# One order of ScalarE and VectorE work in a decoding step, and one more raw weight tile: attention with two feed-forward products on one core

## The chip, the cores and the metric

The kernel runs on one core of one Trainium2 chip. The core has TensorE for matmuls, VectorE and ScalarE for element-wise work, GpSimd, and SyncE, whose queue here issues all DMAs. Each engine takes its own instructions in the order in which the program puts them into its queue and waits on semaphores for the others. The metric is device time in microseconds (us) of one execution; lower is better.

## The reference

```python
x = softmax(q @ k^T / 8, causal) @ v          # 2 x 12 heads, 448 positions, 64 wide
x = x.reshape(896, 768)                       # tokens x model
h = max(x @ w1, x @ w2, x @ w3)               # 768 x 768 each
x2 = h @ w_out                                # 768 x 768
g = s * relu(x2 @ w_in) ** 2 + b              # 768 x 2048
out = g @ w_out2                              # 2048 x 768
```

q, k and v are float32. The weights are float64; the kernel gets their 64-bit words and makes a float32 value of each word itself.

## The kernel before

**Stages.** Attention works through 24 heads, a pair of heads at a time; `emit(t)` puts out the work of head `t` together with later work of the heads before it, in the order of the list `ORDER`. Then `moe()` follows: 36 products `x @ w1..w3` of 128 x 448 outputs (the first of them, `early_product`, is done during the last attention heads), 12 products `h @ w_out` (the x2 stage), 32 products `x2 @ w_in` (the g stage), and the output stage, line 559, with seven accumulators of 128 x 384 at a time, twice. A product is 6 x 3 matmuls of 448 columns (line 453): each operand is split into a high and a low part, and high x high, high x low and low x high are summed. Eight PSUM banks go round among the products; the output accumulators take the same eight in turn.

**Weight tiles.** There are 56, each 128 x 768. A tile goes through these operations: the DMA `wraw` (line 114); on ScalarE `wa` (line 133) and `wr` (line 134), which take the high and the low word apart; on VectorE two clamps (lines 137 and 140), then the rounding (lines 146 and 151); on ScalarE `whi` (line 156), the high part; on VectorE `wlo`, the difference (helper in line 86). Buffers: two for raw tiles, two for `wa`, two for `wr`, three for `whi` and `wlo`. A new raw tile is fetched into the buffer that line 146 has just read.

**Steps.** The decoding is cut into steps. `begin()` is called seven times in attention (at the heads in `STEPS`) and then once in each product, ahead of its last six-th of matmuls, and once for each f of the output stage. A call first puts out what is due from the products before it, then `decode()`. An even step ends with the rounding of one tile and `wa`, `wr` of the next; an odd step has `whi` and `wlo` of one tile and the clamps of the next. So one tile is started every two steps, and a product pair uses one tile.

**What is due in the g stage.** A product's evacuation is spread over the three steps that follow it: `relu` on ScalarE (line 544) from PSUM into `r`; then `stt` on VectorE (line 533), r = max(p, 0) * r, `ident` on ScalarE (line 536), s * r + b, and `copy` on ScalarE (line 539), the high part of g; then `sub` on VectorE (line 86), its low part. The buffers `r` come from the pool `tmp`, four in number. A step puts out the oldest first: `sub`, `stt`, `ident`, `copy`, `relu`. I use these names below: `wa`, `wr`, `whi`, `wlo`, clamps, rounding, and `sub`, `stt`, `ident`, `copy`, `relu`.

**SyncE's queue.** In attention it issues, for each pair of heads, the loads R and V, the store and the spread of the softmax sums (`rcd`, `rb`), and four copies QK; the first two raw tiles are fetched behind the head t = 17 (`FETCH`).

Of the kernel before, what the change touches and what calls it, by code (L numbers as in the profile page):

```python
# [27 lines left out]
)  # L28


FETCH = 17
STEPS = (19, 20, 21, 23, 24, 25, 27)
EARLY = {24: 2, 25: 2, 26: 1, 27: 1}

# [9 lines left out]
def kernel(  # L44
# [14 lines left out]
    nc = tc.nc  # L59
# [14 lines left out]
    const = ctx.enter_context(tc.tile_pool(name="const", bufs=1))  # L74
    x_p = ctx.enter_context(tc.tile_pool(name="x", bufs=KD))
    w_p = ctx.enter_context(tc.tile_pool(name="w", bufs=3))
    wr_p = ctx.enter_context(tc.tile_pool(name="wr", bufs=2))
    wa_p = ctx.enter_context(tc.tile_pool(name="wa", bufs=2))
    wd_p = ctx.enter_context(tc.tile_pool(name="wd", bufs=2))

    ident = const.tile([128, 128], F32, name="ident")
    sb = const.tile([128, 2], F32, name="sb")
    ones = const.tile([128, 512], mybir.dt.bfloat16, name="ones")

    def sub_lo(eng, lo, full, hi):
        eng.tensor_tensor(out=lo, in0=full, in1=hi.bitcast(F32), op=ALU.subtract)  # L86
# [8 lines left out]
    now = [0]  # L95
# [1 line left out]
    def after(steps, fn):  # L97
        due.setdefault(now[0] + steps, []).append((-steps, fn))

    def begin(enter=True):  # L100
        for _, fn in sorted(due.pop(now[0], []), key=lambda e: e[0]):
            fn()
        decode(enter)
        now[0] += 1

    step = begin

    w_src, raws, ready, stages = [], [], [], []

    def fetch_w():  # L110
        if w_src:
            src = w_src.pop(0)
            raw = wr_p.tile([128, DM], I64, tag="wraw", name="wraw")
            nc.sync.dma_start(out=raw, in_=src)
            raws.append(raw)

    def decode(enter=True):


        for fns in [s.pop(0) for s in stages]:  # L120
            for fn in fns:
                fn()
        while stages and not stages[0]:
            stages.pop(0)
        if not (enter and raws) or now[0] % 2:
            return
        raw = raws.pop(0)
        words = raw.bitcast(I32).rearrange("p (n t) -> p n t", t=2)
        low, high = (words[:, :, n] for n in range(2))
        a = wa_p.tile([128, DM], I32, tag="wa", name="wa")  # L130
        r = wd_p.tile([128, DM], I32, tag="wr", name="wr")
        f = a.bitcast(F32)
        nc.scalar.activation(out=f, in_=high.bitcast(F32), func=ACTF.Abs)  # L133
        nc.scalar.activation(out=r, in_=low.bitcast(U32), func=ACTF.Copy, scale=2.0 ** -29)  # L134

        def clamped():
            nc.vector.tensor_scalar(  # L137
                out=f, in0=f, scalar1=UNDER, scalar2=OVER, op0=ALU.max, op1=ALU.min
            )
            nc.vector.tensor_scalar(  # L140
                out=a, in0=a, scalar1=3, scalar2=0x3FFFFFF8,
                op0=ALU.logical_shift_left, op1=ALU.bitwise_and,
            )

        def rounded():
            nc.vector.scalar_tensor_tensor(  # L146
                out=a, in0=high, scalar=-0x40000000, in1=a,
                op0=ALU.bitwise_and, op1=ALU.bitwise_or,
            )
            fetch_w()  # L150
            nc.vector.tensor_tensor(out=a, in0=a, in1=r, op=ALU.add)  # L151

        def split():
            hi = w_p.tile([128, DM], F32R, tag="whi", name="whi")
            lo = w_p.tile([128, DM], F32R, tag="wlo", name="wlo")
            nc.scalar.copy(out=hi, in_=f)  # L156
            sub_lo(nc.vector, lo, f, hi)
            ready.append((hi, lo))

        stages.append([[clamped], [rounded], [split]])  # L160

    def next_w():
        return ready.pop(0)
# [6 lines left out]
    def attention():  # L170
        with ExitStack() as c2:
            pool = lambda n, b, **kw: c2.enter_context(tc.tile_pool(name=n, bufs=b, **kw))
            mask = pool("mk", 1).tile([CH, S], F32, name="mask")
            ld = pool("ld", 3)
            vp = pool("vp", 6)
# [204 lines left out]
            def emit(t):  # L380
# [47 lines left out]
                if t in EARLY:  # L428
                    ops["M"] = lambda: [next(first, None) for _ in range(EARLY[t])]
                ops["W"] = lambda: [begin() for at in STEPS if at == t]  # L430
                for n in ORDER[h]:
                    if n in ops:
                        ops[n]()

            for t in range(n_heads + 4):
                emit(t)
                if t == FETCH:
                    fetch_w()
                    fetch_w()
            for _ in first:  # L440
                pass


    t_p = ctx.enter_context(tc.tile_pool(name="tmp", bufs=4))
    early = {}

    def cols(dst, a, b):
# [125 lines left out]
    with tc.manual_schedule():  # L573
        attention()
        moe()
# [50 lines left out]
```

## Time and profile before

| | |
|---|---|
| runs, median (lowest to highest) | 565.22 us (563.42 to 567.94) |
| profiled execution | 562.34 us, its span 560.3 us |
| TensorE (PE) busy | 534.4 us, 95%; weight loads (PEld) 82% |
| VectorE (DVE), ScalarE (ACT), GpSimd (POOL) busy | 62%, 52%, 8% |
| mean granted TensorE clock | 0.991 |

The span runs from the first to the last instruction. A page of the profile gives busy shares for the whole span; which engine sets the pace in a stretch is read from views of that stretch: its busy time, the chain of waits that ended last, and the timeline of single instructions. In the timeline's rows the engine is named by its short name, L156 is line 156, and what stands in brackets is how long the engine stood idle before the row, and whose end released it.

### The profile page before, as it was taken

The page shows a single profiled execution, that of the slowest core. Times are in us where ns is not written, and L with a number is a line of the kernel's source. Part 1 is how long each engine was busy: PE and PEld are TensorE (multiplying, and loading weights), DVE is VectorE, ACT ScalarE, POOL GpSimd, SP SyncE. Part 2 cuts the span into 40 slices and gives each one's busy share as a digit, 9 for nine tenths or more (in the row PEclk, how much of TensorE's full clock was granted, in tenths as well). Part 3 has the DMA queues.
Part 4 walks back from the last instruction along what each step waited for, and adds up shares of the span by engine and source line. Part 5 has one row for each costly group of instructions (what it writes and reads, how often), then busy time and mean ns, then how long its engine had stood idle before and what let it go on. Part 6 is the DMA issues. An engine that isn't in the chain of part 4 may idle for free.

```text
span 560.3 us, 7507 instructions
## 1 busy us (share of the span) xinstructions
PE 534.4 (95%) x2788; PEld 457.8 (82%) x2789; DVE 348.1 (62%) x653; ACT 292.4 (52%) x574; POOL 47.2 (8%) x43
## 2 busy tenths in 40 slices
PE   8999999979999999999999999989887599999997
PEld 4666666558999999999999999867676599999997
DVE  5465566767757757667666575766757675556501
ACT  3777777954335344434444756657575643334201
POOL 3143535122000000000000000000000000000000
PEclk9999999999999999999999999999999699999999
DMA  8987877523333333233323322323132243253102
GB/s 205 214 245 193 220 183 239 160 85 114 113 112 113 112 113 113 73 124 107 104 105 109 114 70 100 94 75 112 57 113 61 109 135 125 99 191 117 54 0 99
DMA packets 21108, 68.43 MB, mean 122 GB/s; under 512 B 3088, under 2 KB 9744, under 8 KB 21072
## 3 DMA queue, kind: packets, MB, share of 16 engines
q1 hardware_dynamic: 21072, 67.95, 39.2%
q8 instruction: 22, 0.36, 0.3%
q14 instruction: 14, 0.11, 0.1%
HBM read 55.05 MB, written 2.80 MB: 103 GB/s over the span
## 4 chain that ended last, share of the span: by engine, by line
PE 71%; ACT 17%; DVE 8%; issue 2%; DMA 1%; SPq 0%; ACTq 0%
PE m L453 31%; PE m L559 21%; PE s L244 9%; PE t L309 5%; PE o L324 4%; ACT r L536 4%; ACT g L539 3%; DVE wlo L86 3%; ACT r L544 2%; ACT wa L133 2%; ACT wr L134 2%; ACT whi L156 2%; DVE g L86 2%; DVE r L533 2%; DVE wa L137 1%
## 5 line engine op out<-in xcount | busy, mean ns | idle before, releaser
L453 PE MATMUL m<-x,whi 128*128 128x448 f32 x816 | 233.1, 367 | 6.9 <-ACT whi L156 5.6
L453 PEld LDWEIGHTS m<-x,whi 128*128 128x128 f32 x816 | 152.3, 188 | 22.8 <-ACT whi L156 8.5
L453 PE MATMUL m<-x,wlo 128*128 128x448 f32 x408 | 149.9, 367 | 2.5 <-DVE wlo L86 2.5
L559 PE MATMUL m<-whi,g 128*128 128x384 f32 x448 | 116.7, 340 | 7.8 <-DVE r L533 7.0
L86 DVE TENSOR_TENSOR wlo<-wa,whi 128x768 fp32r<-128x768 f32 x56 | 53.8, 960 | 112.0 <-ACT whi L156 112.0
L559 PEld LDWEIGHTS m<-whi,g 128*128 128x128 f32 x448 | 82.5, 191 | 9.3 <-DVE r L533 8.1
L453 PEld LDWEIGHTS m<-x,wlo 128*128 128x128 f32 x408 | 76.6, 188 | 11.6 <-DVE wlo L86 5.6
L559 PE MATMUL m<-wlo,g 128*128 128x384 f32 x224 | 75.9, 339 | 0.5 <-DVE wlo L86 0.5
L133 ACT ACTIVATE wa<-wraw 128x768 f32<-128x768 f32 x56 | 51.0, 912 | 38.8 <-DMA wraw<-in_w_dram 22.7
L156 ACT CAST whi<-wa 128x768 fp32r<-128x768 f32 x56 | 46.6, 832 | 33.7 <-PE m L559 29.1
L252 DVE CUSTOM_DVE_ANT_0 s<-s,mask 112x224 f32<-112x224 f32 (+1 forms) x96 | 43.5, 455 | 27.2 <-PE s L244 26.2
L260 ACT ACTIVATE P<-s,mx 112x224 f32<-112x224 f32 (+1 forms) x96 | 46.9, 495 | 18.4 <-DVE mx L252 16.0
L151 DVE CUSTOM_DVE_ANT_0 wa<-wa,wr 128x1536 uint16<-128x1536 uint16 x56 | 54.7, 977 | 1.9
L146 DVE SCALAR_TENSOR_TENSOR wa<-wraw,wa 128x768 int32<-128x768 int32 x56 | 53.4, 953 | 0.6
L536 ACT ACTIVATE r<-r,sb 128x448 f32<-128x448 f32 x32 | 24.2, 758 | 50.0 <-DVE r L533 50.0
L134 ACT ACTIVATE wr<-wraw 128x768 int32<-128x768 uint32 x56 | 50.2, 896 | 0.0
L559 PEld LDWEIGHTS m<-wlo,g 128*128 128x128 f32 x224 | 42.8, 191 | 0.8 <-DVE wlo L86 0.8
L453 PE MATMUL m<-h,whi 128*128 128x448 f32 x144 | 40.9, 365 | 0.0
L397 ACT COPY PT<-t 112x336 f32<-112x336 f32 (+1 forms) x72 | 31.5, 477 | 12.0 <-PE t L309 12.0
L244 PE MATMUL s<-HL 64*112 64x224 f32 (+3 forms) x112 | 37.6, 364 | 0.2 <-DVE HL L86 0.2
L309 PE MATMUL t<-ident,P 112*112 112x112 f32 x240 | 32.8, 268 | 0.1
L244 PE MATMUL s<-QK 128*112 128x224 f32 (+1 forms) x88 | 32.7, 371 | 0.0
(48 smaller groups left out, 481.2 us busy)
## 6 DMA issues: line engine op xcount, KB each, us to landing
wraw<-in_w_dram SPq DMA_DIRECT2D x56, 768.0 KB
QK<-HL SPq DMA_DIRECT2D x44, 224.0 KB
R<-in_qk_dram SPq DMA_DIRECT2D x11, 448.0 KB
V<-in_v_dram SPq DMA_DIRECT2D x12, 224.0 KB
rb<-rcd SPq DMA_DIRECT2D x24, 112.0 KB
out_dram<-o SPq DMA_DIRECT2D x14, 192.0 KB
R<-in_qk_dram SPq DMA_DIRECT2D x2, 224.0 KB
rcd<-rows SPq DMA_DIRECT2D x12, 3.5 KB
```

Of the source, the lines that this page charges most:

```text
L86: eng.tensor_tensor(out=lo, in0=full, in1=hi.bitcast(F32), op=ALU.subtract)
L133: nc.scalar.activation(out=f, in_=high.bitcast(F32), func=ACTF.Abs)
L134: nc.scalar.activation(out=r, in_=low.bitcast(U32), func=ACTF.Copy, scale=2.0 ** -29)
L146: nc.vector.scalar_tensor_tensor(out=a, in0=high, scalar=-0x40000000, in1=a, op0=ALU.bitwise_and, op1=ALU.bitwise_or,)
L151: nc.vector.tensor_tensor(out=a, in0=a, in1=r, op=ALU.add)
L156: nc.scalar.copy(out=hi, in_=f)
L244: nc.tensor.matmul(ps[:, o:o + n], lhsT, rhs, start=(m == 0), stop=(m == len(terms) - 1))
L260: nc.scalar.activation(out=s_t["P"][:, poff[i]:poff[i] + n], in_=ps[:, o:o + n], func=ACTF.Exp, bias=s_t["mx"][:, i:i + 1], scale=-1.0, ac ...
L309: nc.tensor.transpose(ps[0:CH, o:o + CH], head[t]["P"][:, a:a + CH], ident[0:CH, 0:CH])
L453: nc.tensor.matmul(p, wt[w][:, ws], cols(act[i], a, b), start=(i == 0 and n == 0), stop=(i == len(act) - 1 and n == 2),)
L536: nc.scalar.activation(out=r, in_=r, func=ACTF.Identity, scale=sb[:, 0:1], bias=sb[:, 1:2])
L559: nc.tensor.matmul(acc[t][:, 0:EH], gt[f][:, a, ts], w[:, ws], start=(f == 0 and n == 0), stop=(f == KG - 1 and n == 2),)
```

## The change

In `decode()`, ScalarE's part of a step (`whi` of an odd step; `wa` and `wr` of an even one) is now put out ahead of what is due, and VectorE's part behind it as before, the newest tile first. So in an odd step the clamps now stand ahead of `wlo`. There are three raw buffers in place of two, and the first three raw tiles are fetched one by one behind the heads 16, 18 and 20. The pool `tmp` has three buffers in place of four, and the tile `ones` lies in attention's own space.

```diff
-FETCH = 17
+FETCH = (16, 18, 20)
...
-    wr_p = ctx.enter_context(tc.tile_pool(name="wr", bufs=2))
+    wr_p = ctx.enter_context(tc.tile_pool(name="wr", bufs=3))
...
-    def begin(enter=True):
+    def begin():
+        back = [f for f in [s.pop(0)() for s in stages] if f]
+        while stages and not stages[0]:
+            stages.pop(0)
+        if raws and now[0] % 2 == 0:
+            enter()
         for _, fn in sorted(due.pop(now[0], []), key=lambda e: e[0]):
             fn()
-        decode(enter)
+        for fn in reversed(back):
+            fn()
         now[0] += 1
...
-    def decode(enter=True):
-
-
-        for fns in [s.pop(0) for s in stages]:
-            for fn in fns:
-                fn()
-        while stages and not stages[0]:
-            stages.pop(0)
-        if not (enter and raws) or now[0] % 2:
-            return
+    def enter():
         raw = raws.pop(0)
...
             nc.scalar.copy(out=hi, in_=f)
-            sub_lo(nc.vector, lo, f, hi)
-            ready.append((hi, lo))
-
-        stages.append([[clamped], [rounded], [split]])
+
+            def low_part():
+                sub_lo(nc.vector, lo, f, hi)
+                ready.append((hi, lo))
+
+            return low_part
+
+        stages.append([lambda: clamped, lambda: rounded, split])
...
             for t in range(n_heads + 4):
                 emit(t)
-                if t == FETCH:
-                    fetch_w()
+                if t in FETCH:
                     fetch_w()
...
-    t_p = ctx.enter_context(tc.tile_pool(name="tmp", bufs=4))
+    t_p = ctx.enter_context(tc.tile_pool(name="tmp", bufs=3))
```

ScalarE's queue in the g stage, before, from the `whi` of an odd step over the even step to the next odd one's `whi` (a number behind a name tells one buffer's use from the next):

```order
L156 CAST whi_3683<-wa_3589 128x768
L536 ACTIVATE r_3661<-r_3661,sb_74 128x448
L539 CAST g_3628<-r_3661 128x448
L544 ACTIVATE r_3692<-m_3662 128x448
L133 ACTIVATE wa_3719<-wraw_3651 128x768
L134 ACTIVATE wr_3720<-wraw_3651 128x768
L536 ACTIVATE r_3692<-r_3692,sb_74 128x448
L539 CAST g_3628<-r_3692 128x448
L544 ACTIVATE r_3726<-m_3694 128x448
L156 CAST whi_3748<-wa_3654 128x768
```

The same queue and place now (the lines have moved by four: L152 is `whi`, L129 and L130 are `wa` and `wr`):

```order
L152 CAST whi_3684<-wa_3586 128x768
L536 ACTIVATE r_3633<-r_3633,sb_74 128x448
L539 CAST g_3569<-r_3633 128x448
L544 ACTIVATE r_3667<-m_3635 128x448
L129 ACTIVATE wa_3716<-wraw_3596 128x768
L130 ACTIVATE wr_3717<-wraw_3596 128x768
L536 ACTIVATE r_3667<-r_3667,sb_74 128x448
L539 CAST g_3634<-r_3667 128x448
L544 ACTIVATE r_3698<-m_3668 128x448
L152 CAST whi_3749<-wa_3651 128x768
```

The kinds follow one another as before. What moved is the place among the products: before, `ident`, `copy` and `relu` that follow `whi` belong to the next, even step, and now to the same odd step as `whi` (`whi_3684` and `relu` of product `m_3635` in place of `whi_3683` and `m_3662`, the product behind it). Likewise `wa`, `wr` now stand at the head of the even step and stood at its end.

VectorE's queue in the g stage, before, from the `wlo` of an odd step on:

```order
L86 TENSOR_TENSOR wlo_3229<-wa_3134,whi_3228 128x768
L137 TENSOR_SCALAR wa_3199<-wa_3199 128x768
L140 TENSOR_SCALAR wa_3199<-wa_3199 128x768
L86 TENSOR_TENSOR g_3108<-r_3172,g_3108 128x448
L533 SCALAR_TENSOR_TENSOR r_3206<-m_3174,r_3206 128x448
L146 SCALAR_TENSOR_TENSOR wa_3199<-wraw_3131,wa_3199 128x768
L151 ISA wa_3199<-wa_3199,wr_3200 128x1536
```

And now (L85 is the helper, L133 and L136 the clamps, L142 and L147 the rounding):

```order
L133 TENSOR_SCALAR wa_3196<-wa_3196 128x768
L136 TENSOR_SCALAR wa_3196<-wa_3196 128x768
L85 TENSOR_TENSOR wlo_3230<-wa_3131,whi_3229 128x768
L85 TENSOR_TENSOR g_3114<-r_3178,g_3114 128x448
L533 SCALAR_TENSOR_TENSOR r_3212<-m_3180,r_3212 128x448
L142 SCALAR_TENSOR_TENSOR wa_3196<-wraw_3076,wa_3196 128x768
L147 ISA wa_3196<-wa_3196,wr_3197 128x1536
```

The clamps and `wlo` have changed places; `sub` and `stt` and the rounding stand where they stood. On SyncE's queue the raw tiles behind heads 16, 18 and 20 now stand ahead of the spread `rb` and the QK copies of the next head; from the moe stages on the order is the same, each fetch two steps earlier with respect to the tile's use.

## Rows read from the trace of the kernel before

**Rows 1.** Chain that ended last, 120 to 305 us: start, us, what.

```profile
120.64 4.45 DMA wraw<-in_w_dram
...
127.34 175.39 PE m L453 x864
```

**Rows 2.** Timeline of ScalarE, g stage: start, us, engine, line, operation, [idle before].

```profile
311.63 0.82 ACT L156 CAST whi<-wa 128x768 fp32r<-128x768 f32 x1
315.61 0.76 ACT L536 ACTIVATE r<-r,sb 128x448 f32<-128x448 f32 x1 [3.16 <-DVE r L533]
316.41 0.57 ACT L539 CAST g<-r 128x448 fp32r<-128x448 f32 x1
316.88 0.54 ACT L544 ACTIVATE r<-m 128x448 f32<-128x448 f32 x1
317.32 0.89 ACT L133 ACTIVATE wa<-wraw 128x768 f32<-128x768 f32 x1
318.11 0.90 ACT L134 ACTIVATE wr<-wraw 128x768 int32<-128x768 uint32 x1
...
320.60 0.82 ACT L156 CAST whi<-wa 128x768 fp32r<-128x768 f32 x1
```

**Rows 3.** Timeline of VectorE in the same loop.

```profile
312.48 0.96 DVE L86 TENSOR_TENSOR wlo<-wa,whi 128x768 fp32r<-128x768 f32 x1 [2.94 <-ACT whi L156]
313.36 0.56 DVE L137 TENSOR_SCALAR wa<-wa 128x768 f32<-128x768 f32 x1
313.95 0.56 DVE L140 TENSOR_SCALAR wa<-wa 128x768 int32<-128x768 int32 x1
314.43 0.62 DVE L86 TENSOR_TENSOR g<-r,g 128x448 fp32r<-128x448 f32 x1
314.96 0.62 DVE L533 SCALAR_TENSOR_TENSOR r<-m,r 128x448 f32<-128x448 f32 x1
315.50 0.95 DVE L146 SCALAR_TENSOR_TENSOR wa<-wraw,wa 128x768 int32<-128x768 int32 x1
316.48 0.96 DVE L151 CUSTOM_DVE_ANT_0 wa<-wa,wr 128x1536 uint16<-128x1536 uint16 x1
```

**Rows 4.** Timeline of TensorE: first wait of the g stage, output stage.

```profile
358.33 0.47 PE L453 MATMUL m<-x,wlo 128*128 128x448 f32 x1 [0.31 <-DVE wlo L86]
...
429.04 0.45 PE L559 MATMUL m<-whi,g 128*128 128x384 f32 x1 [0.81 <-ACT whi L156]
...
441.11 0.69 PE L559 MATMUL m<-whi,g 128*128 128x384 f32 x1 [4.83 <-DVE r L533]
...
556.43 0.34 PE L559 MATMUL m<-whi,g 128*128 128x384 f32 x1
```

**Rows 5.** Stretches: length, busy PE, PEld, DVE, ACT, POOL, granted clock, DMA, GB/s.

```profile
365.00:380.00 15.00, 12.88 (x60) 10.51 (x59) 10.65 (x16) 8.58 (x15) 0.00 (x0) 1.00 0.16 53
440.00:455.00 15.00, 13.89 (x68) 13.89 (x69) 11.30 (x17) 8.70 (x12) 0.00 (x0) 0.82 0.30 105
450.00:550.00 100.00, 100.00 (x578) 100.00 (x578) 50.35 (x65) 31.43 (x39) 0.00 (x0) 1.00 0.29 101
```

**Rows 6.** Timeline of several engines, end of attention.

```profile
116.75 0.96 DVE L86 TENSOR_TENSOR wlo<-wa,whi 128x768 fp32r<-128x768 f32 x1 [2.62 <-ACT whi L156]
...
118.69 0.16 DVE L401 TENSOR_SCALAR su<-su 112x8 f32<-112x8 f32 x1
119.15 0.26 PE L282 MATMUL t<-ident,su 112*8 112x112 f32 x1 [2.83 <-DVE su L404]
...
125.18 0.91 ACT L133 ACTIVATE wa<-wraw 128x768 f32<-128x768 f32 x1 [2.75 <-DMA wraw<-in_w_dram]
...
127.34 0.68 PE L453 MATMUL m<-x,whi 128*128 128x448 f32 x2 [1.39 <-ACT t L462]
```

**Rows 7.** Timeline of SyncE and TensorE: QK of pair 10, issue and first use.

```profile
84.82 3.06 SPq L217 DMA_DIRECT2D QK<-HL  x4
...
95.89 0.34 PE L244 MATMUL s<-QK 128*112 128x224 f32 x1
```

More of the change, by code (lines that the diff above doesn't have):

```diff
@@ L82 @@
     sb = const.tile([128, 2], F32, name="sb")
-    ones = const.tile([128, 512], mybir.dt.bfloat16, name="ones")
     def sub_lo(eng, lo, full, hi):
@@ L98, in after @@
         due.setdefault(now[0] + steps, []).append((-steps, fn))
-    def begin(enter=True):
+    w_src, raws, ready, stages = [], [], [], []
+    def begin():
[4 more added lines that the diff above has]
+            enter()
         for _, fn in sorted(due.pop(now[0], []), key=lambda e: e[0]):
             fn()
-        decode(enter)
+        for fn in reversed(back):
+            fn()
         now[0] += 1
     step = begin
-    w_src, raws, ready, stages = [], [], [], []
     def fetch_w():
@@ L172, in attention @@
             pool = lambda n, b, **kw: c2.enter_context(tc.tile_pool(name=n, bufs=b, **kw))
+            ones = pool("on", 1).tile([128, 512], mybir.dt.bfloat16, name="ones")
             mask = pool("mk", 1).tile([CH, S], F32, name="mask")
```

## The prediction

> **What bounds the kernel now.** I read the page first (busy shares and slices), then the busy time by stretches, the chain of waits and, for the stretch where the chain leaves TensorE, the timelines of ScalarE and VectorE. The page says that TensorE is busy 95% of the span, so what can be won is the rest, and the question is where it lies.
>
> The chain answers it. From 127.34 us it is on TensorE alone for 864 matmuls, 0.2030 us each [rows 1]. That holds to 302.73 us, the entry to the g stage (the products `x2 @ w_in`). From there to 441 us the chain runs through ScalarE and VectorE in one repeating piece, two steps long: `whi`, `wlo`, the clamps, `stt` (line 533), `ident` (line 536), `copy` (539), `relu` (544), `wa`, `wr`, `ident`, `copy`, `relu`, `whi` [rows 2, 3]. Add the distances from start to start: `whi` to `wlo` 0.85, `wlo` 0.88, clamps 1.07 (0.59 + 0.48), `sub` 0.53, `stt` to `ident` 0.65, `ident`-`copy`-`relu` 1.71 (0.80 + 0.47 + 0.44), `wa` 0.79 and `wr` 0.80, the second `ident`-`copy`-`relu` 1.69; sum 8.97 us, which is the distance of the two `whi` at 311.63 and 320.60 [rows 2, 3]. TensorE needs 36 matmuls x 0.2030 = 7.31 us for the same two products. The loop is 1.66 us too slow, and it is slow by hand-over: ScalarE stands still 3.16 us in each loop, until `stt` [rows 2], and VectorE 2.94 us, until `whi` [rows 3].
>
> TensorE doesn't feel this at once, since weights and PSUM banks are ahead: its first wait of the stage is at 358.33 us [rows 4], 55.6 us or 6.2 loops after 302.73, so the lead is 6.2 x 1.66 = 10 us. After that it waits in every loop, and at the change to the output stage (line 559) for 4.83 us in one piece, behind which a matmul takes 0.69 us instead of 0.34 [rows 4]. The granted clock of 440 to 455 us is 0.82, that of 450 to 550 is 1.00 [rows 5]: behind the gap the engine runs for a while at 1.2 instead of 2.4 GHz.
>
> **What the gaps cost, counted by matmuls.** Products: 79 from 127.34 on, x 18 matmuls x 0.2030 = 288.7 us; the output stage starts at 429.04 [rows 1, 4], 301.7 us later. Lost: **13.0 us**. Output: 672 matmuls; 578 touch the 100 us of the window, about 2 of them at its edges, so 0.1736 us each [rows 5], 116.7 us in all; from 429.04 to the last matmul's end at about 556.6 [rows 4] are 127.6 us. Lost: **10.9 us**, low clock included.
>
> Idle time alone gives less: in 365 to 380 us the row has 2.12 us without a matmul, but 60 matmuls where 73.9 fit [rows 5], so 2.8 us are missing. The Trainium skill (Perfetto Trace Analysis, Identifying the Most-Contended Engine) says the same as a rule: matmul busy share is a poor measure, since pipelined instructions look smaller in the trace than they are. By idle time this sum would shrink by about a quarter, to 18 us instead of 23.9; the trace is on the side of the count.
>
> **The change, part by part.**
>
> *ScalarE's order.* No instruction is added or removed. In the g stage `whi` (odd steps) and `wa`, `wr` (even steps) move from behind `ident`, `copy`, `relu` to ahead of them. VectorE's clamps and rounding stay behind its other work, and only `wlo` and the clamps change places. Follow the new loop with the same distances, from `stt` of an odd step at 0, with no wait for TensorE. ScalarE: `ident` 0.65, `copy` 1.45, `relu` 1.92, free at 2.36. VectorE: clamps from 0.53, `wlo` 1.60 to 2.56 without a wait, because `whi` stood ahead of `ident`. Even step: `wa` waits for the buffer that `wlo` reads (a new wait) until 2.59, `wr` 3.38, `ident` 4.18 (its `stt` starts at 3.01 and is no obstacle), `copy` 4.96, `relu` 5.43. VectorE meanwhile rounds, 3.54 to 5.48. Then ScalarE's `whi` from 5.87; VectorE's `sub` when `copy` ends, 5.53, and `stt` at 6.06. The loop is **6.1 us**, under TensorE's 7.31. The lead isn't used up, nothing on TensorE is late, and the next thing to wait is ScalarE for TensorE, which costs nothing. A loop of up to 7.31 + 10/16 = 7.9 us would still cost nothing in the 16 loops of the stage.
>
> At the change of stage the seventh accumulator takes the bank of the last product but one. TensorE gets there 18 x 0.1736 = 3.1 us after the last product's end; with the engines in step, that bank's `stt` runs near that end. So the 4.83 us go, and the low clock with them. I take 13.0 + 10.9 = **23.9 us**. Bounds: nothing, if the loop stays at 8.97; 23.9 is all there is.
>
> *The new waits.* `wa` now stands ahead of `ident` and can be held by a raw tile not yet there or by `wlo`; queued behind it are `ident`, `copy`, `relu`, and VectorE's next `sub` and `stt` wait for those. In the sum it is held 0.23 us a loop (2.36 to 2.59).
>
> *VectorE's swap at the start.* At t = 23 `wlo` waits 2.62 us for `whi`, the clamps follow, and only then, at 118.69, the softmax sums, for whose transpose TensorE waits 2.83 us [rows 6]. With the clamps done in that wait the sums come 1.06 us sooner. *Third raw tile:* at 125.18 `wa` has waited 2.75 us for a transfer that could start only when VectorE let go of the buffer (4.45 us in the chain [rows 1]), and the evacuation behind it holds TensorE 1.39 us at 127.34 [rows 6]. With three tiles that raw is there long before; `wa` is then held by `wlo`, so I count some 0.5 of the 1.39. Together **1.6 us**; bounds 0 (the last attention head's x tile, made by GpSimd, could set the pace) and 1.06 + 1.39 = 2.45.
>
> *The early fetches.* The one after t = 16 goes on SyncE's queue ahead of the spread of the sums and the four QK copies, which were issued from 84.82 on for 3.06 us and are first read at 95.89 [rows 7]. A raw tile's 4.45 us [rows 1] fit in those 8 us: cost 0. Without that cover it is at most 4.45 us.
>
> *`tmp` 4 to 3, `ones` moved:* 0. The buffer that `relu` gets was last read by `sub` of three products before, one step earlier. The cover is that step; if it were gone, `relu` would wait one `sub`, 0.53 us.
>
> Sum: 560.3 - 23.9 - 1.6 = 534.8 us of span, and with the 2.0 us around it 536.8, against 562.34 of the profiled execution. The runs' median lies 2.9 us above that execution (565.22), so I forecast 536.8 + 2.9 = **540 us**.
>
> **The rivals.**
> *Part of it only.* The loop falls, but to between 7.9 and 8.97. Each 0.1 us above 7.9 costs 16 x 0.1 = 1.6 us; at 8.4 that is 8 us and most of the change of stage stays clean: 543 to 553. For it: `wa`'s new wait on `wlo`, and distances taken from a loop with pauses in it. Against: from 6.1 to 7.9 are 1.8 us of room.
> *The early raw fetch collides with QK.* TensorE waits up to 4.45 us near 96 us: 544. Against: the 8 us.
> *It doesn't do what it says.* Another loop of 9 us takes over, and only the start is won: 563. Against: the loop above has no such sum.
> *Slower: the head of ScalarE's queue blocks.* Place: `wa` in even steps, `whi` in odd ones. If each is held until VectorE has finished its whole step, the two engines alternate: ScalarE's 5.8 us (0.82 + 1.59 + 1.71 + 1.69) and VectorE's 5.9 us of a loop in a row, 11.7 us. It decides from 8.97 on: at 9.5, 16 x 0.53 = 8.5 us more, less the start's 1.6, 572; at 11.7, some 44 us more, 607. The Trainium skill (TensorE: Matmul & The Clock Gate, Architectural detail) bears on it: ScalarE and VectorE take their queues strictly in order, so whatever is held at the head holds all behind it. The trace agrees on the queue as it is, `wlo` holding the clamps, `sub` and `stt` for 2.94 us [rows 3]. Against the rival: VectorE is through with an odd step 2.56 us behind the start of its `stt`, and ScalarE with its three at 2.36, so the head is held for 0.2 us and not for a step.
>
> **How the numbers follow.** Forecast 0.68 (536 to 543, the start's bounds and the runs' spread); part only 0.17; collision 0.08; no effect 0.04; slower 0.03. The first three hold 0.93 and reach from 536 to 553; 1 us is left below for the start's upper bound, so the range is 535 to 553. About 1% is what a measurement of this kernel can tell from no change: faster by more 0.93, within 0.04, slower 0.03.
>
> **What would show it.** Right: the chain stays on TensorE from about 125 us to the end but for single waits; no wait of line 453 for `whi` or `wlo`; VectorE's waits of `wlo` for `whi` all but gone; granted clock 1.00 at the change of stage; output stage from about 414 us. Wrong: a loop above 7.31 us in the g stage, idle ScalarE ahead of `wa` or `whi` with VectorE as releaser, TensorE idle near 96 us, or a wait of line 559 for line 533.

## The result, and the profile after

The changed kernel takes 540.65 us (median; 538.33 to 543.30) against 566.08 us of the kernel before in the same call; the ratio is 0.9556 with a 95% interval of 0.9495 to 0.9616. Its profiled execution took 540.73 us, with a span of 538.4 us. Medians below are over all runs of a call, while the ratios leave out runs that took more than 1.5% over the fastest of their kernel.

The chain of waits that ended last; start us, us, what (it answers [rows 1], and what of it stood between 303 and 441 us on ScalarE and VectorE is gone):

```profile
129.86 288.46 PE m L453 x1422
418.32 116.52 PE m L559 x672
```

TensorE goes from the first of the 79 products to the last matmul of the output stage without a break: 0.2029 us for each of 1,422 matmuls and 0.1734 for each of 672. All that TensorE waited for in the whole execution (line, for whom: us, times, longest):

```profile
PE t L283 <- DVE su L405: 1.8, 1, 1.8
PE warm L355 <- DVE ones L361: 1.5, 1, 1.5
PE m L453 <- ACT t L462: 1.4, 1, 1.4
```

None is in the g stage or behind it. Two of the stretches of [rows 5] again, and the change to the output stage in place of the third (length; busy PE, PEld, DVE, ACT, POOL; granted clock; DMA; GB/s):

```profile
365.00:380.00 15.00, 15.00 (x76) 13.91 (x75) 12.66 (x19) 12.26 (x19) 0.00 (x0) 1.00 0.30 105
418.00:433.00 15.00, 15.00 (x88) 14.99 (x87) 10.35 (x15) 7.00 (x11) 0.00 (x0) 1.00 0.45 152
440.00:455.00 15.00, 15.00 (x89) 15.00 (x88) 7.63 (x10) 5.33 (x7) 0.00 (x0) 1.00 0.29 105
```

The first had 60 matmuls and has 76; the granted clock stays at 1.00 through the change of stage, which now comes 11 us sooner. The loop of the g stage on ScalarE (it answers [rows 2]):

```profile
345.83 0.83 ACT L152 CAST whi<-wa 128x768 fp32r<-128x768 f32 x1
346.63 0.76 ACT L536 ACTIVATE r<-r,sb 128x448 f32<-128x448 f32 x1
347.43 0.57 ACT L539 CAST g<-r 128x448 fp32r<-128x448 f32 x1
349.04 0.55 ACT L544 ACTIVATE r<-m 128x448 f32<-128x448 f32 x1 [1.05 <-PE m L453]
349.48 0.89 ACT L129 ACTIVATE wa<-wraw 128x768 f32<-128x768 f32 x1
350.27 0.93 ACT L130 ACTIVATE wr<-wraw 128x768 int32<-128x768 uint32 x1
351.07 0.76 ACT L536 ACTIVATE r<-r,sb 128x448 f32<-128x448 f32 x1
...
352.69 0.55 ACT L544 ACTIVATE r<-m 128x448 f32<-128x448 f32 x1 [0.26 <-PE m L453]
353.13 0.83 ACT L152 CAST whi<-wa 128x768 fp32r<-128x768 f32 x1
```

From `whi` to `whi` are 7.30 us, TensorE's own pace. ScalarE no longer waits for `stt`; it waits for TensorE's products, 1.05 + 0.26 = 1.31 us in each loop. That is the room, and the prediction had 7.31 - 6.1 = 1.2. VectorE in the same loop (it answers [rows 3]):

```profile
346.51 0.55 DVE L133 TENSOR_SCALAR wa<-wa 128x768 f32<-128x768 f32 x1
347.10 0.56 DVE L136 TENSOR_SCALAR wa<-wa 128x768 int32<-128x768 int32 x1
347.57 0.95 DVE L85 TENSOR_TENSOR wlo<-wa,whi 128x768 fp32r<-128x768 f32 x1
348.44 0.62 DVE L85 TENSOR_TENSOR g<-r,g 128x448 fp32r<-128x448 f32 x1
349.62 0.62 DVE L533 SCALAR_TENSOR_TENSOR r<-m,r 128x448 f32<-128x448 f32 x1 [0.56 <-ACT r L544]
```

`wlo` starts without a wait, where it had stood idle for 2.94 us.

### The profile page after: what moved, and what is told of

The parts are those of the page before. It is cut to its first block, busy times and chain, and to the rows that moved or that the text cites. A ratio compares the mean times of both kernels' runs of the same rounds, so it can differ in the third digit from the quotient of the medians.

```text
span 538.4 us, 7535 instructions
## 1 busy us (share of the span) xinstructions
PE 530.1 (98%) x2789; PEld 459.1 (85%) x2789; DVE 350.8 (65%) x653; ACT 297.4 (55%) x574; POOL 47.3 (9%) x43
## 4 chain that ended last, share of the span: by engine, by line
PE 97%; DVE 1%; ACT 1%; issue 0%; ACTq 0%
PE m L453 54%; PE m L559 22%; PE s L245 10%; PE t L310 5%; PE o L325 4%; PE warm L355 2%; DVE wlo L85 1%; PE t L283 0%; ACT PT L398 0%; ACT P L261 0%; ACT wa L129 0%; DVE wa L142 0%; DVE wa L136 0%; ACT wr L130 0%; ACT whi L152 0%
## 5 line engine op out<-in xcount | busy, mean ns | idle before, releaser
L559 PE MATMUL m<-whi,g 128*128 128x384 f32 x448 | 114.0, 334 | 0.0
L152 ACT CAST whi<-wa 128x768 fp32r<-128x768 f32 x56 | 46.7, 834 | 65.1 <-PE m L559 43.8
L129 ACT ACTIVATE wa<-wraw 128x768 f32<-128x768 f32 x56 | 50.9, 909 | 57.4 <-DVE wlo L85 57.4
L559 PEld LDWEIGHTS m<-whi,g 128*128 128x128 f32 x448 | 80.8, 188 | 0.0
L85 DVE TENSOR_TENSOR wlo<-wa,whi 128x768 fp32r<-128x768 f32 x56 | 54.3, 970 | 38.7 <-ACT whi L152 38.7
L559 PE MATMUL m<-wlo,g 128*128 128x384 f32 x224 | 74.8, 334 | 0.0
L253 DVE CUSTOM_DVE_ANT_0 s<-s,mask 112x224 f32<-112x224 f32 (+1 forms) x96 | 43.5, 455 | 29.4 <-PE s L245 28.5
L147 DVE CUSTOM_DVE_ANT_0 wa<-wa,wr 128x1536 uint16<-128x1536 uint16 x56 | 54.7, 977 | 1.9
L142 DVE SCALAR_TENSOR_TENSOR wa<-wraw,wa 128x768 int32<-128x768 int32 x56 | 53.2, 951 | 0.0
L130 ACT ACTIVATE wr<-wraw 128x768 int32<-128x768 uint32 x56 | 50.6, 904 | 0.0
L460 DVE TENSOR_TENSOR t<-t,m 128x448 f32<-128x448 f32 x24 | 14.9, 621 | 39.1 <-PE m L453 39.1
L245 PE MATMUL s<-HL 64*112 64x224 f32 (+3 forms) x112 | 39.3, 386 | 0.0
L136 DVE TENSOR_SCALAR wa<-wa 128x768 int32<-128x768 int32 x56 | 32.4, 579 | 1.9
```

The lines of the kernel that those rows point to most:

```text
L142: nc.vector.scalar_tensor_tensor(out=a, in0=high, scalar=-0x40000000, in1=a, op0=ALU.bitwise_and, op1=ALU.bitwise_or,)
L245: nc.tensor.matmul(ps[:, o:o + n], lhsT, rhs, start=(m == 0), stop=(m == len(terms) - 1))
L253: nc.vector.tensor_tensor_reduce(out=ps[:, o:o + n], in0=ps[:, o:o + n], in1=mask[:, S - n:S], scale=-scale, scalar=BIG, op0=ALU.add, op1= ...
L559: nc.tensor.matmul(acc[t][:, 0:EH], gt[f][:, a, ts], w[:, ws], start=(f == 0 and n == 0), stop=(f == KG - 1 and n == 2),)
```

## The experiments

The theory: the 24 us are the hand-over loop of the g stage, and ScalarE's order alone removes it. Rivals: the third raw tile does it, since ScalarE had waited for transfers; or VectorE's swap does. All ratios are to the kernel before, run on the same chip in the same call; the diffs are to the changed kernel.

**The raw tiles alone** (all else of the change too, but both parts of a step behind what is due):

```diff
+        for _, fn in sorted(due.pop(now[0], []), key=lambda e: e[0]):
+            fn()
         back = [f for f in [s.pop(0)() for s in stages] if f]
         while stages and not stages[0]:
             stages.pop(0)
+        for fn in back:
+            fn()
         if raws and now[0] % 2 == 0:
             enter()
-        for _, fn in sorted(due.pop(now[0], []), key=lambda e: e[0]):
-            fn()
-        for fn in reversed(back):
-            fn()
```

> Three raw tiles, the early fetches, tmp 3 and the moved tile as in the change, but both engines' parts of a step stand where they stood before. Theory (the gain is the hand-over loop of the g stage): the loop stays at 8.97 us, the time within 1.5 us of before; the only thing won is up to 0.8 us at the end of attention. Rival (raw tiles that come late hold ScalarE, 22.7 us of its waits before were for them): most of the gain is here, 541 to 548 us.

565.43 us, ratio 1.0013 (0.9978 to 1.0048): nothing. TensorE's waits are those of before; line, for whom: us, times, longest, the first two rows of the kernel before and the other two of this run:

```profile
PE m L559 <- DVE r L533: 7.0, 2, 4.8
PE m L453 <- ACT whi L156: 5.6, 7, 0.8
```

```profile
PE m L559 <- DVE r L533: 6.8, 2, 4.7
PE m L453 <- ACT whi L152: 5.4, 7, 0.8
```

Not even the end of attention gains. `wa` no longer waits there for a transfer, but TensorE waits the same 1.39 us as in [rows 6], now for another:

```profile
127.28 0.62 DVE L340 TENSOR_TENSOR xf<-o,rb 128x448 f32<-128x448 f32 x1 [1.01 <-DMA rb<-rcd]
...
128.05 0.65 PE L453 MATMUL m<-x,whi 128*128 128x448 f32 x2 [1.39 <-DVE xf L340]
```

VectorE's last division by the softmax sums (`xf`) waits for the spread of the sums, `rb`, and holds the PSUM bank that the first product wants.

**The order alone, with two raw tiles:**

```diff
-FETCH = (16, 18, 20)
+FETCH = (17, 17)
...
-    wr_p = ctx.enter_context(tc.tile_pool(name="wr", bufs=3))
+    wr_p = ctx.enter_context(tc.tile_pool(name="wr", bufs=2))
...
-                if t in FETCH:
+                for _ in range(FETCH.count(t)):
                     fetch_w()
```

> The change's order on both engines, but two raw tiles, both fetched behind head 17. Theory: g stage clean, within 1 us of the changed kernel, 540 to 542 us. Rival (three raw tiles are needed, since wa now stands at the head of ScalarE's queue and would be held by the transfer): TensorE waits in the g stage again, 548 us or more.

539.16 us, just under the range expected; the ratio, 0.9553 (0.9496 to 0.9611), is the changed kernel's own. Products and output stage take 288.47 and 116.50 us. So the third tile is not needed even with `wa` at the head of the queue: 2.91 us of waiting for a transfer remain at the end of attention, where TensorE's wait is 1.53 us instead of 1.44.

**ScalarE's order alone** (`wlo` ahead of the clamps again):

```diff
-        for fn in reversed(back):
+        for fn in back:
```

> ScalarE's part ahead as in the change, but VectorE does wlo ahead of the clamps, as before. Theory: the g stage's loop has room enough either way, so TensorE waits for nothing there; the 1.06 us at the softmax sums of the end of attention are lost again: 541 to 542.5 us. Rival (the swap on VectorE is what frees the loop): well above 545 us.

541.54 us (539.75 to 548.10), 0.9576 (0.9516 to 0.9637). The g stage is clean (288.46 us for 1,422), and TensorE's wait for the sums is back at 2.83 us. The theory stands: ScalarE's order suffices for the 24 us.

**VectorE's swap alone** (ScalarE's part behind what is due, as before):

```diff
+        for _, fn in sorted(due.pop(now[0], []), key=lambda e: e[0]):
+            fn()
         back = [f for f in [s.pop(0)() for s in stages] if f]
         while stages and not stages[0]:
             stages.pop(0)
-        if raws and now[0] % 2 == 0:
-            enter()
-        for _, fn in sorted(due.pop(now[0], []), key=lambda e: e[0]):
-            fn()
         for fn in reversed(back):
             fn()
+        if raws and now[0] % 2 == 0:
+            enter()
```

> ScalarE's part behind what is due, as before; only VectorE's swap (clamps ahead of wlo). The clamps, 1.07 us, leave the loop: 8.97 - 1.07 = 7.9 us. By the prediction's words a loop of 7.9 costs nothing: 540 to 541.5 us. The other reading: 16 loops lag 16 x (7.9 - 7.31) = 9.4 us at the end of the g stage, the accumulators must wait until the last but one product is evacuated, only some 5.7 us of that lag are covered there, and behind the gap the clock is low: 4 to 6 us more, 544.5 to 547 us, with no wait for whi or wlo inside the stage.

546.81 us, 0.9678 (0.9622 to 0.9733). ScalarE's loop, from one `ident` of an odd step to the next, and what TensorE meets at the change of stage:

```profile
379.39 0.77 ACT L536 ACTIVATE r<-r,sb 128x448 f32<-128x448 f32 x1 [2.10 <-DVE r L533]
...
387.32 0.76 ACT L536 ACTIVATE r<-r,sb 128x448 f32<-128x448 f32 x1 [2.10 <-DVE r L533]
```

```profile
421.98 0.44 PE L559 MATMUL m<-whi,g 128*128 128x384 f32 x1 [1.07 <-DVE r L533]
...
426.97 0.69 PE L559 MATMUL m<-whi,g 128*128 128x384 f32 x1 [4.19 <-DVE r L533]
```

```profile
427.00:430.00 3.00, 3.00 (x9) 3.00 (x10) 2.97 (x5) 2.97 (x5) 0.00 (x0) 0.50 0.31 72
```

The loop is 7.93 us, as the sum had it. No weight is late inside the stage, yet the time isn't the changed kernel's: the lag of 16 x (7.93 - 7.30) = 10 us stands at the end of the stage, the accumulators wait 1.07 and 4.19 us for `stt`, and behind the gap the granted clock is 0.50, the level of 1.2 GHz. From 418.12 us on, the output stage takes 123.9 us where it needs 116.5, 7.4 lost: 5.3 in the two waits, and the rest mostly where the clock is low. So of the 10 us of lag about 5 were covered. The second reading holds, and the prediction's falls.

**More work on the loop.** Each `copy` of the g stage twice, and four times (k = 1 and 3):

```diff
-                        nc.scalar.copy(out=cols(g, 0, b), in_=r)
+                        for _ in range(k + 1):
+                            nc.scalar.copy(out=cols(g, 0, b), in_=r)
```

> The changed kernel with each copy of the g stage done twice (the second writes the same values), so 0.47 us more of ScalarE's time in each step, on the loop: 6.1 becomes some 6.8 us, still under TensorE's 7.31. Theory (the loop has 1.2 us of room): no loss, within 1 us of the changed kernel, no wait of TensorE in the g stage. Rival (the loop is at its limit already): 0.7 us in each of 16 loops, 11 us more, some 551.

537.57 us (537.27 to 545.94), 0.9468 (0.9403 to 0.9532): nothing lost, 288.46 us for the 1,422. The two copies and the `relu` behind them in its trace:

```profile
349.03 1.17 ACT L540 CAST g<-r 128x448 fp32r<-128x448 f32 x2
350.10 0.54 ACT L545 ACTIVATE r<-m 128x448 f32<-128x448 f32 x1
```

Two copies take 1.07 us up to `relu`, where one took 0.47 [rows 2]. So 0.60 us came on in each step, more than the 0.47 expected, and 1.2 in each loop, and it fits: the room of 1.2 to 1.3 us is there.

> The changed kernel with each copy of the g stage done four times, 3 x 0.47 us more in each step: the loop becomes some 8.6 us. With the lag of 16 x (8.6 - 7.31) = 20.6 us, less the 2.5 us by which the loss stayed under the lag in the kernel with VectorE's swap alone (9.9 us of lag, 7.4 lost), 18 us more than the changed kernel: 557 to 560 us, with waits for whi and wlo in the second half of the stage and a wait for line 533 at its end. By the prediction's words (free up to 7.9, then 1.6 us for each 0.1): 11 us more, 551 to 552.

567.77 us, 1.0023 (0.9981 to 1.0064), as slow as the kernel before and 9 us over my number. A loop in its trace, from `ident` to `ident` two steps on, with the four copies as one row:

```profile
375.30 0.77 ACT L536 ACTIVATE r<-r,sb 128x448 f32<-128x448 f32 x1
376.10 2.37 ACT L540 CAST g<-r 128x448 fp32r<-128x448 f32 x4
...
384.79 0.76 ACT L536 ACTIVATE r<-r,sb 128x448 f32<-128x448 f32 x1
```

The loop is 9.49 us, not 8.6: four copies into one place take 2.28 us up to `relu` (376.10 to 378.38), so each of the three further ones 0.60 and not 0.47, and ScalarE now has hardly any idle time but is full. The lag is 16 x (9.49 - 7.30) = 35 us, the loss against the execution with one more copy 564.9 - 535.5 = 29.4 us of span; with products starting at 127.08 and 127.02 us the two compare well. The kind is as expected, TensorE waits 7.9 us for `wlo` and 7.6 for line 533. The size follows the measured loop only roughly: by the expectation's own rule (the lag less 2.5 us) it would be 32.5 us.

**The end of attention.** The evacuation of the early product ahead of the last attention step's `wa`, `wr`:

```diff
-EARLY = {24: 2, 25: 2, 26: 1, 27: 1}
+EARLY = {24: 2, 25: 2, 26: 1, 27: 2}
```

> The changed kernel, with the evacuation of the early product (t, line 462) put out ahead of the last attention step's wa and wr. Theory (at the end of attention wa, held by wlo, holds this evacuation, and TensorE waits 1.4 us for it): the wait falls to some 0.6 us, the distance from the softmax sums' transpose to the first matmul of the feed-forward products from 8.26 to 7.4 us; the time is 0.8 us less. Rival (the last x tile on GpSimd sets the pace): the wait reappears for x, no gain.

543.89 us, 0.9594 (0.9525 to 0.9662), not less but more. The end of attention did what it should in part: from the sums' transpose to the first product 7.83 us instead of 8.26; the wait left, 1.03 us, is for `xf`, whose `rb` is late by 1.00 us. But the products then took 294.11 us, and all four runs lie between 543.05 and 546.06 us. That is taken up below. With head 23's `whi` earlier as well:

```diff
                 for n in ORDER[h]:
+                    if t == 23 and n == "Ec":
+                        ops.pop("W")()
                     if n in ops:
```

> As the one before, and whi of head 23's step ahead of the last exponential of that head, so that wlo ends sooner and the softmax sums follow at once. Theory: TensorE's wait for the sums' transpose falls from 1.8 to about 0.5 us, so another 1.2 us less; in all some 2 us less than the changed kernel, 538 to 539 us. Rival: what whi delays on ScalarE (the last exponential, by 0.75 us, and with it the sums) gives the same wait back.

537.98 us (536.16 to 543.65), 0.9494 (0.9416 to 0.9572). TensorE's wait for the sums falls from 1.77 us to 0.31 (the products' line is 455 in this kernel):

```profile
117.48 0.26 PE L283 MATMUL t<-ident,su 112*8 112x112 f32 x1 [0.31 <-DVE su L405]
125.30 0.64 PE L455 MATMUL m<-x,whi 128*128 128x448 f32 x2 [1.00 <-DVE xf L340]
```

**The same kernels again,** for what differed between executions:

> The changed kernel once more, beside the two that follow. Open: why its profiled execution reached the feed-forward products at 129.86 us and three other kernels with the same head of the program at 126.84 to 128.05. Theory (an execution's own: the clock rises sooner or later in the first 13 us): this time the first 40 matmuls may run at either clock, and the products start near 127 or near 130 us, with nothing else different behind. Rival (the changed kernel's own): near 130 again.

537.91 us, 0.9511 (0.9466 to 0.9555); the products start at 127.18 us, not 129.86.

> The kernel with the early evacuation once more. It had taken 294.1 us for the 1,422 matmuls of 448 columns where all others took 288.4 to 288.5, at the same granted clock. Theory (an execution's or a chip's own state): 288.5 us this time in the profile, or 294 in another kernel of this call, and the time about 1 us under the changed kernel's. Rival (this kernel's own): 294 us again, and 3 to 5 us over the changed kernel.

538.25 us, 0.9501 (0.9457 to 0.9546). The products of this one kernel in two executions, chains of waits of the first and of the second:

```profile
126.42 294.11 PE m L453 x1422
```

```profile
127.91 288.43 PE m L453 x1422
```

So the slower pace isn't the kernel's. All four executions of the first call took 543.05 to 546.06 us and all four of the second, on another chip, 536.40 to 538.77, so it may have lasted through a whole call; what it belongs to is open.

> The kernel with both edits at the end of attention once more, with more rounds. Theory: about 2 us under the changed kernel on the same chip, ratio to before near 0.950. Rival: what it wins at the end of attention is lost to the spread between executions, same as the changed kernel within 1 us.

538.92 us (535.50 to 545.16), 0.9499 (0.9455 to 0.9542), against 537.91 us and 0.9511 of the changed kernel on the same chip. The profiled execution was the one of 545.16 us, and it ran its products at the slower pace again, where the same program had needed 288.43 us in its first call:

```profile
128.62 294.11 PE m L455 x1422
```

By its traces this version starts the products 1.2 us ahead of the changed kernel, not 2: at 128.62 us against 129.86, the pace at the start having risen late in both; of the 1.9 us between 125.30 and 127.18, the two with an early rise, 0.8 stand already at 11 us, where the changed kernel happened to wait longer for its first exponentials. By the times it can't be told from the changed kernel.

## Why the prediction was right

**The loop and the gaps.** 301.7 us to the output stage became 288.5, and 127.6 us of output stage became 116.5: 13.2 and 11.1 us, where the count by matmuls had said 13.0 and 10.9. The count was the right one; by idle time it would have been 18 us. The idle time was too small because the busy time held too much, 12.88 us for 60 matmuls [rows 5], 0.215 each where the full pace is 0.203; so the reason quoted in the prediction, instructions that look smaller than they are, is not what these rows show. The mechanism is shown by the two halves: raw tiles alone give nothing, ScalarE's order alone all of it. VectorE's swap alone wins 17 us of the 24: the 13 within the products (288.3 us to the output stage), but only 3.7 of the 11 behind them.

**The change of stage.** No wait, clock 1.00, as forecast. The step that failed is a side remark, on which no term of the sum rests: a loop of 7.9 us "would still cost nothing", and the rival "part of it only" with a clean change of stage. VectorE's swap alone makes just such a loop and costs some 7 us: what lag the weights hide inside the stage is paid at its end, where the accumulators need the banks. The bound that counts is TensorE's own 7.31, with about 5 us of lag covered in all (10 us of lag, 5.3 us of waits), not 10.

**The new waits.** ScalarE's `wa` waits 57.4 us for `wlo` in all, 16.0 before, and none of it reaches TensorE but one at the end of attention, below. The slower rival, the blocked head, is off: the room is 1.31 us a loop, and one more copy in each step fits in.

**The start.** The swap gave what it should: TensorE's wait for the sums' transpose fell from 2.83 us to 1.77, the 1.06 of the sum. The 0.5 us from the raw tile did not come; the step that was mis-sized is "`wa` is then held by `wlo`". Rows of the changed kernel:

```profile
125.53 1.32 POOL L85 TENSOR_TENSOR x<-xf,x 128x448 fp32r<-128x448 f32 x1
125.78 1.88 DVE L85 TENSOR_TENSOR wlo<-wa,whi 128x768 fp32r<-128x768 f32 x1
127.70 0.90 ACT L129 ACTIVATE wa<-wraw 128x768 f32<-128x768 f32 x1 [2.81 <-DVE wlo L85]
129.29 0.52 ACT L462 COPY t<-m 128x448 f32<-128x448 f32 x1
129.86 0.67 PE L453 MATMUL m<-x,whi 128*128 128x448 f32 x2 [1.44 <-ACT t L462]
```

Behind the clamps `wlo` now starts 0.25 us behind GpSimd's subtraction and takes 1.88 us, where it takes 0.95 elsewhere. So `wa` is held for 2.81 us, as long as it had been by the transfer, and not for the 1.16 us that `wlo` held it in the run with the raw tiles alone; TensorE waits 1.44 us for the evacuation behind it. The Trainium skill (SBUF — State Buffer, Who interferes with whom) has a rule for it: a VectorE instruction with two SBUF inputs contends with a GpSimd instruction that reads SBUF. These rows agree, 1.88 against 0.95 us. The two had met before the change as well, in the other order:

```profile
122.47 1.09 DVE L86 TENSOR_TENSOR wlo<-wa,whi 128x768 fp32r<-128x768 f32 x1 [0.37 <-ACT whi L156]
122.84 1.71 POOL L86 TENSOR_TENSOR x<-xf,x 128x448 fp32r<-128x448 f32 x1
```

There it was GpSimd's subtraction that took longer. All 13 traces keep to this: with `wlo` first, 1.09 us and 1.71 to 1.75 for the subtraction (three traces); with `wlo` second, 1.88 to 1.90 and 1.31 to 1.33 (ten). So the swap that won 1.06 us at the sums also put `wlo` behind the clamps and behind GpSimd's subtraction. That the evacuation was held by the queue's head is shown by moving it ahead. But then `xf` and its late `rb` are next, as with the raw tiles alone, and some 1.0 us of the wait stays; so of the raw tile's 1.39 us little could be won either way.

**The early fetches** cost nothing: no wait of TensorE near 96 us.

**The sum.** 534.8 us of span were forecast, 538.4 came, 3.6 more; 535.7 in the second profile of the same kernel. The 2.7 between the two arise in the first 14 us, told below: the third group of warm-up matmuls starts at 13.94 us in the first and at 11.25 in the second. Of the 0.9 that stay, 0.5 is the raw tile that didn't come, and 0.8 is the start again: before the change that group started at 10.41 us, and ahead of it TensorE waited 1.22 us in the second profile for ScalarE's first exponentials. The gaps gave 0.4 more than forecast. That the median, 540.65, lies within 0.7 us of the forecast is in part luck: 2.9 us had been added for the distance of the runs from a profiled execution, and there was none this time (540.65 and 540.73), so that it made up for most of the 3.6 us of the sum. On another chip the same kernel took 537.91 us.

## What to carry to other kernels

Where two engines hand a chain to each other, add the start-to-start distances round the loop and compare the sum with the pace of the engine that should be full: neither of the two need be busy for the loop to be too slow, and putting the work that depends on nothing new ahead of the work that waits takes it off the loop, here at no cost inside the stage. Count what gaps cost by matmuls that are missing at the full pace, not by idle time, and don't spend a lead twice: lag hidden within a stage falls due where the next stage needs the buffers. Ahead of calling a transfer late, look for what would hold the same instruction if the transfer came early.

## What the runs showed of the hardware that was not expected

The kernel with the early evacuation, on the same inputs, ran its matmuls of 448 columns at 0.2068 us in one execution and at 0.2028 in another (294.11 and 288.43 us for 1,422), at a granted clock of 1.00 in both, from the first product to the last; the output matmuls of 384 columns kept their 0.1734. The kernel with both edits did the same, with the same two numbers. Each pace was seen on both chips. The cause is open. It is 5.7 us, more than most edits here.

One and the same wait did or didn't cost clock. Behind TensorE's wait for the softmax sums, 2.83 us with ScalarE's order alone (first row) and 1.77 with one more copy (second row), the granted clock was 0.50, the level of 1.2 GHz, for some 3 us; behind the same 2.83 us in the kernel before (third row) and the same 1.77 in the changed kernel's second profile (fourth row) it stayed at 1.00. Columns as in [rows 5]:

```profile
121.00:124.00 3.00, 3.00 (x9) 1.00 (x7) 2.60 (x4) 1.08 (x2) 0.99 (x2) 0.50 0.58 143
```

```profile
119.00:122.00 3.00, 3.00 (x9) 1.20 (x7) 2.93 (x5) 1.91 (x4) 0.85 (x2) 0.50 0.48 140
```

```profile
120.00:123.00 3.00, 3.00 (x15) 1.77 (x13) 2.60 (x4) 1.35 (x3) 0.73 (x2) 1.00 0.37 108
```

```profile
120.00:123.00 3.00, 3.00 (x16) 1.60 (x14) 2.93 (x5) 1.81 (x4) 0.94 (x2) 1.00 0.52 159
```

From the sums' transpose to the first product the two took 8.96 and 8.99 us, where these others took 8.19 and 8.25.

The pace at the program's start rises at different times: nine warm-up matmuls of 512 columns at about 8 us took 4.02 us in the changed kernel's first profile (the first row) and 2.12 in its second (the second row), though TensorE had been busy from 1.46 us on in both. That is about half the pace, as the lower clock level would give, but the granted clock reads 1.00 from 8 to 10 us in both, so the clock is inferred here and not shown.

```profile
8.76 4.02 PE L355 MATMUL warm<-ones 128*128 128x512 bf16 x9
```

```profile
7.17 2.12 PE L355 MATMUL warm<-ones 128*128 128x512 bf16 x9
```

It moves everything behind it by 2.7 us, and it isn't the kernel's: the products started at 129.86 and at 127.18 us with one and the same program.
